# Reordering ScalarE's squares, copies and casts in the first stage of a fused recurrence and mixture-of-experts kernel

## The chip, the cores and the metric

The kernel runs on one NeuronCore of a Trainium2 chip. The metric is the device time of one execution in microseconds (us), taken as the median of several executions.

## The reference

A linear recurrence with complex decay feeds a mixture of experts that is normalised by eight rounds over rows and columns. Shapes: batch 4, 8 heads, 768 positions, head size 48; 3072 tokens of width 384, 8 experts with 1024 hidden units.

```python
scale = np.minimum(mag, 0.999) / (mag + 1e-06)      # mag = |a|
for t in range(S):
    new_re = ar * S_re - ai * S_im
    new_im = ar * S_im + ai * S_re
    S_re, S_im = (new_re + einsum('bhd,bhe->bhde', k_t, v_t), new_im)
    y[:, :, t] = einsum('bhd,bhde->bhe', q_t, S_re)
...
logits = x @ w_gate                                  # x is y with the heads side by side
P = np.exp(logits - logits.max())
for _ in range(8):
    P /= P.sum(1, keepdims=True) + 1e-09
    P /= P.sum(0, keepdims=True) + 1e-09
    P *= N / E
for e in range(E):
    out += P[:, e:e + 1] * (np.maximum(x @ w1[e], 0.0) @ w2[e])
```

## The kernel before, in words

The 3072 tokens are cut into 12 blocks of 256 (two chunks of 128 each; `SUB`, `CH`). The kernel has two stages. The first one (`phase1` and the start of `phase2a`, to about 610 us) computes the recurrence block by block and beside it the experts 0 and 1; the second (`phase2b`) the other six experts for all tokens. The change touches the first stage alone.

For each block i, `elem(i)` prepares the decay on ScalarE and VectorE: `chain` takes a *first square* (L520, with a sum), two roots and squares (L526, L527, L530) with VectorE steps between (L525 to L533), `scan` forms running products (L437 to L442, VectorE), and then a *second square* (L541), a root and its square (L545, L547), and VectorE steps (L543, L550 to L554) scale keys (kh) and queries (z). The blocks 0 to 2 do this in two halves, the others in one piece. The scaled tensors go through DMAs (L577: keys on SP, queries on GpSimd's queue) into the layouts `ks` and `qs`.

`mix(i)` is the recurrence over a block. TensorE transposes keys (ktp, L597; copied to `kts` by ScalarE, L598), multiplies them with queries (sp, L624; masked by VectorE into `sc`, L627), forms the state's increment (up, L608; copied by ScalarE as `ut`, L610; turned back as U, L617) and the output y (L641). Small ScalarE copies (rr, rn; L654 to L656) and VectorE steps (L669 to L680) carry the state on. ScalarE casts y to `xh` (L684), VectorE takes the rest `xl` (L685).

While block i goes through `mix`, the experts 0 and 1 run on block i-1, in 16 steps f of 15 matmuls: 9 into `ph` (L256), 6 into the two banks `po` (L217 to L219), which lag three steps behind. ScalarE makes `hh` from ph (L270 for blocks 0 and 1, where TensorE subtracts it again, L273, and ScalarE reads the rest, L274; for the others hh L279 and hf L280, and VectorE's hl, L281). After eight steps ScalarE copies the two banks out (`yst`, L225), and the next expert's first step may write them.

TensorE's order is written out by the program. ScalarE, VectorE, GpSimd and SP get theirs from the framework's scheduler, and the program steers it with edges that hold back an instruction without a wait on the chip: `issue_after(x)` and `add_manual_dep(b, a)` put an instruction behind x or a in the order. Each engine then works strictly in its order.

The gate stands at the end of the first stage, in `phase2a`: logits to P (L718 on GpSimd), a maximum over all (L748, mp L752), and rounds of row sums, a column sum on TensorE (cp, L784, from `spare` of L780) and rescaling (L785 to L793). Between them `more(k)` sends k steps of the last block's experts. Weights for the second stage are prepared there too (`raw` loads, GpSimd's sums L905, ScalarE's and VectorE's parts L942 and L946).

```python
more((4, 4, 2, 2)[k])
...
self.columns(self.psK.tile([128, E], F32, tag="po", name=f"cp{k}"))
```

## Time and profile before

| | |
|---|---|
| median of three executions | 1722.88 us (1721.53 to 1723.43) |
| the profiled execution | 1721.06 us |
| its span in the trace | 1719.3 us (1.76 us lie around it) |
| granted TensorE clock | 0.999 of full speed |

In the page and the views, PE is TensorE, DVE VectorE, ACT ScalarE, POOL GpSimd, SP the queue of loads. L12 is line 12 of the kernel before. In a timeline a row has the start and the length in us, the engine, the line, the operation, what it writes and reads, how many were merged (x2), and in brackets how long the engine sat idle before it and what released it. A wait that the table of waits lists is idle time of TensorE, put down to the instruction that released it. One row can hold merged neighbours, and the lengths of neighbours on one engine overlap a little, so starts say more than lengths.

### The profile page before, as it was taken

The numbers are of one execution on the slowest core, as the hardware profiler recorded it, in microseconds if no ns is written. First come the engines' busy times: TensorE is split into PE (matmuls) and PEld (weight loads), VectorE is DVE, ScalarE is ACT, GpSimd is POOL, SyncE is SP. The second block draws the span as 40 slices with busy tenths as digits, with TensorE's granted clock in tenths as the row PEclk, the third lists the DMA queues.
The fourth block names the chain that finished last, engine by engine and source line by source line (L and its number), as shares of the span: only waits on it lengthen the run. The fifth ranks groups of instructions, "written<-read, shape, count | busy, mean of one in ns | idle before, by whom it ended". The sixth has DMA issues, their size and how long they took to land.

```text
span 1719.3 us, 31262 instructions
## 1 busy us (share of the span) xinstructions
PE 1691.2 (98%) x11824; PEld 1661.2 (97%) x11824; DVE 1262.1 (73%) x2654; ACT 737.7 (43%) x1669; POOL 202.4 (12%) x383
## 2 busy tenths in 40 slices
PE   7999999999999999999999999999999999999998
PEld 5899999999999999999999999999999999999998
DVE  7898999999988787878755666656566655565654
ACT  8555555555543454645433333333433333433331
POOL 4210112111201324242200000000000000000000
PEclk9999999999999999999999999999999999999999
DMA  7434444644448877576577666558666656656560
GB/s 229 134 107 145 118 128 121 167 114 114 115 136 271 350 284 284 213 292 234 199 260 250 224 219 249 192 203 275 226 218 237 205 177 243 232 191 236 192 228 35
DMA packets 160830, 346.02 MB, mean 201 GB/s; under 512 B 15264, under 2 KB 101536, under 8 KB 160672
## 3 DMA queue, kind: packets, MB, share of 16 engines
q1 hardware_dynamic: 155264, 334.03, 56.4%
q0 software_dynamic: 4608, 9.52, 2.5%
q8 instruction: 95, 1.56, 0.4%
q14 instruction: 63, 0.52, 0.1%
q10 hardware_dynamic: 800, 0.39, 0.1%
HBM read 232.53 MB, written 98.70 MB: 193 GB/s over the span
## 4 chain that ended last, share of the span: by engine, by line
PE 67%; DVE 2%; DMA 1%; issue 0%; ACT 0%; POOL 0%; POOLq 0%; SPq 0%; DVEq 0%
PE po L1100 12%; PE po L1098 12%; PE po L1099 12%; PE X L1154 4%; PE X L1155 4%; PE X L1156 4%; PE Y L1154 3%; PE Y L1155 3%; PE Y L1156 3%; PE ph L256 1%; PE V L1154 1%; PE Z L1154 1%; PE V L1156 1%; PE V L1155 1%; PE Z L1155 1%; PE Z L1156 1%
## 5 line engine op out<-in xcount | busy, mean ns | idle before, releaser
L1100 PE MATMUL po<-wd,hl 128*128 128x384 f32 x768 | 257.0, 335 | 0.0
L1099 PE MATMUL po<-wd,hh 128*128 128x384 f32 x768 | 256.6, 334 | 0.0
L1098 PE MATMUL po<-wd,hh 128*128 128x384 f32 x768 | 256.5, 334 | 0.0
L256 PE MATMUL ph<-xh,w 128*128 128x256 f32 x1152 | 226.2, 282 | 1.3 <-ACT xh L684 1.2
L256 PEld LDWEIGHTS ph<-xh,w 128*128 128x128 f32 x1152 | 185.3, 189 | 1.8 <-ACT xh L684 1.8
L256 PE MATMUL ph<-xl,w 128*128 128x256 f32 x576 | 154.4, 282 | 0.0
L1100 PEld LDWEIGHTS po<-wd,hl 128*128 128x128 f32 x768 | 144.2, 188 | 0.8 <-DVE hl L1176 0.2
L1098 PEld LDWEIGHTS po<-wd,hh 128*128 128x128 f32 x768 | 144.2, 188 | 0.0
L1099 PEld LDWEIGHTS po<-wd,hh 128*128 128x128 f32 x768 | 144.2, 188 | 0.0
L279 ACT ACTIVATE hh<-ph 128x256 fp32r<-128x256 f32 x160 | 61.2, 383 | 187.9 <-PE ph L256 187.3
L217 PE MATMUL po<-w,hh 128*128 128x384 f32 x384 | 137.0, 357 | 1.5 <-ACT yst L225 1.5
L219 PE MATMUL po<-w,hl 128*128 128x384 f32 x384 | 129.4, 337 | 0.5 <-DVE hl L281 0.5
L218 PE MATMUL po<-w,hh 128*128 128x384 f32 x384 | 129.1, 336 | 0.0
L1099 PE MATMUL po<-wc,hh 128*128 128x384 f32 x384 | 128.3, 334 | 0.0
L1098 PE MATMUL po<-wc,hh 128*128 128x384 f32 x384 | 128.3, 334 | 0.0
L1100 PE MATMUL po<-wc,hl 128*128 128x384 f32 x384 | 128.3, 334 | 0.0
L577 POOL DMA_DIRECT2D qs<-z x144 | 75.6, 533 | 270.5 <-DVE z L554 74.0
L1175 ACT ACTIVATE hh<-X 128x384 fp32r<-128x384 f32 x64 | 31.5, 492 | 176.1 <-PE X L1156 176.1
L256 PEld LDWEIGHTS ph<-xl,w 128*128 128x128 f32 x576 | 105.7, 189 | 0.0
L1081 DVE SCALAR_TENSOR_TENSOR oa<-po,P,oa 128x384 f32<-128x384 f32 x120 | 72.9, 613 | 20.7 <-PE po L1100 20.5
L281 DVE TENSOR_TENSOR hl<-hf,hh 128x256 fp32r<-128x256 f32 x160 | 68.0, 427 | 11.0 <-ACT hf L280 9.8
L217 PEld LDWEIGHTS po<-w,hh 128*128 128x128 f32 x384 | 72.7, 189 | 2.9 <-ACT yst L225 2.0
(1832 smaller groups left out, 4381.2 us busy)
## 6 DMA issues: line engine op xcount, KB each, us to landing
wd<-wd SPq DMA_DIRECT2D x58, 768.0 KB, 5.8
wa<-wd SPq DMA_DIRECT2D x42, 768.0 KB, 4.5
wb<-wd SPq DMA_DIRECT2D x42, 768.0 KB, 5.8
wc<-wd SPq DMA_DIRECT2D x42, 768.0 KB, 4.5
xP<-xf SPq DMA_DIRECT2D x60, 384.0 KB, 4.5
raw<-in_w_dram SPq DMA_DIRECT2D x12, 1152.0 KB, 8.7
wd<-wc SPq DMA_DIRECT2D x16, 768.0 KB, 4.2
wd<-wa SPq DMA_DIRECT2D x16, 768.0 KB, 4.1
```

Source lines behind the costliest of these rows:

```text
L217: nc.tensor.matmul(po[k], hh[:, s], w2h, start=f == 0, stop=False)
L218: nc.tensor.matmul(po[k], hh[:, s], w2l, start=False, stop=False)
L219: nc.tensor.matmul(po[k], hl[:, s], w2h, start=False, stop=f == NF - 1)
L256: nc.tensor.matmul(ph, w[:, k, ct * 128:ct * 128 + 128], x[:, ct, :], start=q == 0, stop=q == len(terms) - 1)
L577: dma = eng.dma_start(dst[q:q + D - 2:NCT, :, :w], src[:, a, ct * NCH + c, :w])
L1081: V.scalar_tensor_tensor(oa[u, k], p, self.P[:, tt, e:e + 1], oa[u, k], ALU.mult, ALU.add)
L1098: nc.tensor.matmul(po[k], hh[:, s], w2[0], start=c == 1, stop=False)
L1099: nc.tensor.matmul(po[k], hh[:, s], w2[1], start=False, stop=False)
L1100: nc.tensor.matmul(po[k], hl[:, s], w2[0], start=False, stop=c == NF)
L1154: nc.tensor.matmul(ps, w[:, 0, k], x[:, 0], start=start, stop=False, skip_group_check=True)
L1155: nc.tensor.matmul(ps, w[:, 0, k], x[:, 1], start=False, stop=False, skip_group_check=True)
L1156: nc.tensor.matmul(ps, w[:, 1, k], x[:, 0], start=False, stop=True, skip_group_check=True)
```

## The change

The change adds edges for the scheduler. On ScalarE: in block 1's second part (i = 1, n = 5) hh of step 5 goes ahead of the second half of block 1's second square, and one root of block 1 behind hh of step 6; in block 2's (i = 2, n = 3 and 4) the same for steps 3 and 4 of the next expert. The two halves of block 2's first square go behind the last steps of expert 0. The first squares of the blocks 4 and 5 go behind the bank copies yst of expert 1 on the blocks 1 and 2, and their VectorE reader behind VectorE steps of the block before. The second square of block 4 goes behind the cast xh of block 3's second chunk, that of block 10 behind the copy ut of block 9's first chunk, and a root of block 11 behind a bank copy of expert 0 on block 8. In the gate three steps instead of four stand ahead of the first column sum, so that each of the first four column sums stands one step earlier on TensorE, and the memset of `pad` is issued at the end of the rounds.

```diff
@@ -222,7 +222,7 @@
                         st = self.st.tile([128, 2, C], F32R, tag="st", name=f"yst{e}_{i}_{k}").bitcast(F32)[:, 0]
                     else:
                         st = self.xp.tile([128, C], F32, tag="yst", name=f"yst{e}_{i}_{k}")
-                    nc.scalar.activation(st, po[k], AF.Copy)
+                    self.yst[e, i] = nc.scalar.activation(st, po[k], AF.Copy)
                     nc.sync.dma_start(self.ye_d[e][i * NCH + k], st)
 
         while True:
@@ -318,6 +318,7 @@
             nc.gpsimd.memset(t, 0.0)
         self.sb = sb[:, :H * D].rearrange("p (h d) -> p h d", h=H)
         self.xs, self.vt, self.kqd, self.ql, self.sqs, self.zl, self.post = {}, {}, {}, {}, {}, {}, {}
+        self.yst, self.xhc, self.utc = {}, {}, {}
         self.ev, self.dve, self.act, self.root, self.hh, self.hl, self.nthird = [], {}, {}, {}, {}, {}, 0
         ns = self.N // SUB
         self.moe, self.lg, self.mid = self.experts(), None, []
@@ -394,8 +395,12 @@
                 for _ in range(min(len(splits), (0, 1, 2, 2).count(n))):
                     splits.pop(0)()
                 if i == 1 and n == 5:
-                    for a, b in ((self.hl[0, 4], self.post[1][1]), (self.hh[0, 5], self.root[1, 0][1])):
+                    for a, b in ((self.hl[0, 4], self.hh[0, 5]), (self.hh[0, 5], self.post[1][1])):
                         tc.add_manual_dep(b.ins, a.ins.name, edge, reason="step inside the chain")
+                if i == 1 and n == 6:
+                    tc.add_manual_dep(self.root[1, 1][0].ins, self.hf.ins.name, edge, reason="step inside the chain")
+                if i == 2 and n in (3, 4):
+                    tc.add_manual_dep((self.post[2][1] if n == 3 else self.root[2, 1][0]).ins, self.hf.ins.name, edge, reason="step inside the chain")
                 if i == 1 and n == 4:
                     for ins in self.post[1]:
                         tc.add_manual_dep(ins.ins, self.hf.ins.name, edge, reason="chain behind the step")
@@ -414,6 +419,7 @@
                 pairs.append([t[k] for k in range(5) for t in (n0, n1)] + self.dve["m", NCH][:1] + n0[5:] + n1[5:])
                 a0, a1 = self.act[2, 0], self.act[2, 1]
                 pairs.append([t[k] for k in range(4) for t in (a0, a1)])
+                pairs += [[self.hh[0, 7], a0[0]], [self.hh[0, 8], a1[0]]]
                 pairs += [[a1[k], self.hh[0, n]] for k, n in ((1, 12), (2, 13), (3, 14))] + [[a1[2], self.act["kt", 1, 0][0]]]
                 for order in pairs:
                     for a, b in zip(order, order[1:]):
@@ -510,20 +516,25 @@
         base = 2 * ns + ns * NCT * NCH
         z = zt[:, :, :, :CH]
         sq, x, y0, zz = alloc("sq"), alloc("x"), alloc("y0"), alloc("zz")
-        prev = {2: (1, NCH - 1), 3: (2, NCH - 1)}.get(i)
+        prev = (i - 1, NCH - 1 if i <= NHALF else 0) if 1 < i < 6 else None
         for n in parts or [None]:
             f0, f1 = (base + i, base + NHALF + i) if n else (i, ns + i)
             sq_, x_, y_, zz_, z_ = (t if n is None else half(t, n) for t in (sq, x, y0, zz, z))
             with ExitStack() as st:
                 if prev:
                     st.enter_context(tc.issue_after(self.sqs[prev].ins))
+                if i in (4, 5):
+                    st.enter_context(tc.issue_after(self.yst[1, i - 3].ins))
                 act = self.act[i, n or 0] = [nc.scalar.activation(sq_, z_, AF.Square, accum_out=fl[:, f0:f0 + 1])]
             ops = self.dve[i, f"n{n or 0}"] = []
             with ExitStack() as st:
                 if prev:
-                    st.enter_context(tc.issue_after(self.zl[prev[0], 3 - i if i > 2 else 1].ins))
+                    st.enter_context(tc.issue_after((self.zl[prev[0], 3 - i if i > 2 else 1] if i <= NHALF else self.dve[prev][2]).ins))
                 ops.append(V.scalar_tensor_tensor(x_, sq_[:, 0], 1e-20, sq_[:, 1], ALU.max, ALU.add))
-            act.append(nc.scalar.activation(y_, x_, AF.Abs_reciprocal_sqrt))
+            with ExitStack() as st:
+                if i == ns - 1:
+                    st.enter_context(tc.issue_after(self.yst[0, i - 3].ins))
+                act.append(nc.scalar.activation(y_, x_, AF.Abs_reciprocal_sqrt))
             act.append(nc.scalar.activation(zz_, y_, AF.Square, accum_out=fl[:, f1:f1 + 1]))
             ops.append(V.tensor_tensor(x_, x_, zz_, ALU.mult))
             ops.append(V.scalar_tensor_tensor(y_, x_, -3.0, y_, ALU.add, ALU.mult))
@@ -538,7 +549,12 @@
         sq, x, g0, kh = alloc("sq"), alloc("x"), alloc("g0"), alloc("kh")
         for n in parts or [None]:
             sq_, x_, g_, z_, qk_, kh_ = (t if n is None else half(t, n) for t in (sq, x, g0, z, qk, kh))
-            act = nc.scalar.activation(sq_, z_, AF.Square)
+            with ExitStack() as st:
+                if i == 4:
+                    st.enter_context(tc.issue_after(self.xhc[i - 1, NCH - 1].ins))
+                if i == ns - 2:
+                    st.enter_context(tc.issue_after(self.utc[i - 1, 0].ins))
+                act = nc.scalar.activation(sq_, z_, AF.Square)
             self.post.setdefault(i, []).append(act)
             self.dve[i, f"x{n or 0}"] = [V.scalar_tensor_tensor(x_, sq_[:, 0], 1e-26, sq_[:, 1], ALU.max, ALU.add)]
             o = 2 * ns + i * NCT * NCH + (n or 0) * NCT
@@ -607,7 +623,7 @@
                         q = 64 * g
                         nc.tensor.matmul(up[q:q + n, j, :], vt[:, c, lo:lo + n], self.kts[:, 4 * g + j, :], start=True, stop=True, tile_position=(0, q), skip_group_check=True)
                 ut["s"] = tmp.tile([SK, 4, SK], F32, tag="tm", name=f"ut{i}_{c}", bufs=1)
-                nc.scalar.activation(ut["s"], up, AF.Copy)
+                self.utc[i, c] = nc.scalar.activation(ut["s"], up, AF.Copy)
 
             def back(i=i, c=c, ut=ut, lastc=lastc):
                 if lastc:
@@ -681,7 +697,7 @@
                 self.ist = 1 - self.ist
 
             def cast():
-                nc.scalar.activation(xh[:, :, cs], xp, AF.Copy)
+                self.xhc[i, c] = nc.scalar.activation(xh[:, :, cs], xp, AF.Copy)
                 ops.append(nc.vector.tensor_tensor(xl[:, :, cs], xp, xh[:, :, cs].bitcast(F32), ALU.subtract))
 
             if c < NCH - 1:
@@ -990,13 +1006,13 @@
         self.sums(0)
         for nm in FORMS:
             self.swap(0, nm)
-        nc.gpsimd.memset(xa.tile([128, 56], F32, name="pad"), 0.0)
+        pad = xa.tile([128, 56], F32, name="pad")
         self.sinkhorn(xa, more, True)
         for k in range(HEAD):
             self.rows()
             if k == HEAD - 1:
                 break
-            more((4, 4, 2, 2)[k])
+            more((3, 4, 2, 2)[k])
             if k == 2:
                 self.verdict()
                 more(1)
@@ -1008,6 +1024,8 @@
             if k == 0:
                 self.sums(1)
                 self.raw_w(2)
+        with tc.issue_after(self.hf.ins):
+            nc.gpsimd.memset(pad, 0.0)
         more(len(todo))
         self.moe.send((None, None, None))
```

Three places in ScalarE's order show what moves. The numbers behind names are block and chunk (xh4, y4_1, ut9_0) or expert, block and step (hh1_3_7), and the last one is the buffer's; lines of the changed kernel lie 16 further down in `chain` and `mix` behind L541 (L541 becomes L557, L684 becomes L700), L520 becomes L528.

First, ScalarE in block 1's second square, around 71 us; before:

```order
L541 ACTIVATE sq1_884<-z1_777 128x6x128
L274 ACTIVATE hl0_0_4_1023<-ph0_0_4_1012 128x256
L541 ACTIVATE sq1_884<-z1_777 128x6x128
L270 ACTIVATE hh0_0_5_1043<-ph0_0_5_1033 128x256
L545 ACTIVATE g01_886<-x1_885 128x3x128
```

and with the change:

```order
L557 ACTIVATE sq1_884<-z1_777 128x6x128
L274 ACTIVATE hl0_0_4_1023<-ph0_0_4_1012 128x256
L270 ACTIVATE hh0_0_5_1043<-ph0_0_5_1033 128x256
L557 ACTIVATE sq1_884<-z1_777 128x6x128
L561 ACTIVATE g01_886<-x1_885 128x3x128
```

hh of step 5 has moved ahead of the second half of the square.

Second, ScalarE between the last two steps of expert 1 on block 3 and the cast of block 4's second chunk, around 245 us. This place is not named in the change; before:

```order
L545 ACTIVATE g05_3576<-x5_3575 128x768
L546 ACTIVATE fl_82<-x5_3575 128x6
L520 ACTIVATE sq6_4128,fl_82<-z6_4122 128x1536
L547 ACTIVATE g05_3576<-g05_3576 128x768
L279 ACTIVATE hh1_3_7_3403<-ph1_3_7_3393 128x256
L280 ACTIVATE hf1_3_7_3405<-ph1_3_7_3393 128x256
L526 ACTIVATE y06_4130<-x6_4129 128x768
L610 ACTIVATE ut4_1_3421<-up4_1_3412 112x448
L527 ACTIVATE zz6_4131,fl_82<-y06_4130 128x768
L684 ACTIVATE xh4_3165<-y4_1_3342 128x3x128
```

and with the change:

```order
L557 ACTIVATE sq5_3574<-z5_3477 128x1536
L279 ACTIVATE hh1_3_7_3403<-ph1_3_7_3393 128x256
L280 ACTIVATE hf1_3_7_3405<-ph1_3_7_3393 128x256
L626 ACTIVATE ut4_1_3421<-up4_1_3412 112x448
L561 ACTIVATE g05_3576<-x5_3575 128x768
L562 ACTIVATE fl_82<-x5_3575 128x6
L528 ACTIVATE sq6_4128,fl_82<-z6_4122 128x1536
L563 ACTIVATE g05_3576<-g05_3576 128x768
L700 ACTIVATE xh4_3165<-y4_1_3342 128x3x128
L537 ACTIVATE y06_4130<-x6_4129 128x768
```

The second square of block 5 (sq5) stood four rows ahead of the first piece and now stands behind hh of step 6; root, square and root of the blocks 5 and 6 (g05, sq6, g05) stood ahead of hh1_3_7 and now stand between ut and xh; the root and square of block 6 (y06, zz6) now follow xh.

Third, ScalarE around the second chunk of block 9, around 455 us; before:

```order
L541 ACTIVATE sq10_6895<-z10_6798 128x1536
L610 ACTIVATE ut9_0_6509<-up9_0_6500 112x448
L684 ACTIVATE xh9_6372<-y9_0_6386 128x3x128
L545 ACTIVATE g010_6897<-x10_6896 128x768
L546 ACTIVATE fl_82<-x10_6896 128x6
L520 ACTIVATE sq11_7491,fl_82<-z11_7485 128x1536
L547 ACTIVATE g010_6897<-g010_6897 128x768
L279 ACTIVATE hh1_8_1_6555<-ph1_8_1_6545 128x256
L280 ACTIVATE hf1_8_1_6557<-ph1_8_1_6545 128x256
L598 ACTIVATE kts_211<-ktp9_1_0_6574 128x8x48
L598 ACTIVATE kts_211<-ktp9_1_1_6579 128x8x48
L654 ACTIVATE rr1_216<-qs1_196 48x8
```

and with the change:

```order
L626 ACTIVATE ut9_0_6509<-up9_0_6500 112x448
L557 ACTIVATE sq10_6895<-z10_6798 128x1536
L700 ACTIVATE xh9_6372<-y9_0_6386 128x3x128
L279 ACTIVATE hh1_8_1_6555<-ph1_8_1_6545 128x256
L280 ACTIVATE hf1_8_1_6557<-ph1_8_1_6545 128x256
L614 ACTIVATE kts_211<-ktp9_1_0_6574 128x8x48
L561 ACTIVATE g010_6897<-x10_6896 128x768
L562 ACTIVATE fl_82<-x10_6896 128x6
L528 ACTIVATE sq11_7491,fl_82<-z11_7485 128x1536
L614 ACTIVATE kts_211<-ktp9_1_1_6579 128x8x48
L670 ACTIVATE rr1_216<-qs1_196 48x8
L671 ACTIVATE rr1_216<-qs1_196 48x8
```

ut has moved ahead of block 10's second square, and g010 and block 11's first square (sq11) have moved from ahead of hh1_8_1 to a place between the two copies kts. The bank copies yst follow the rows rr and rn in both; before, the root y011 of block 11 stood between them, and now it stands behind hh and hf of the next step.

## Rows read from the trace of the kernel before

**Rows 1.** The page's part 1, busy us (share of the span) and instructions of each engine.
```profile
PE 1691.2 (98%) x11824; PEld 1661.2 (97%) x11824; DVE 1262.1 (73%) x2654; ACT 737.7 (43%) x1669; POOL 202.4 (12%) x383
```

**Rows 2.** The waits of TensorE: waited for, us in total, times, longest us.
```profile
PE mp L752 <- DVE spare L748: 1.7, 1, 1.7
PE ph L273 <- ACT hh L270: 1.6, 2, 0.9
PE po L217 <- ACT yst L225: 1.5, 2, 1.2
PE ph L256 <- ACT xh L684: 1.2, 1, 1.2
PE cp L784 <- DVE spare L780: 1.0, 2, 0.7
...
PE U L617 <- ACT ut L610: 0.6, 1, 0.6
```

**Rows 3.** Busy us (instructions) of PE, PEld, DVE, ACT, POOL, clock, DMA, 250-300 us.
```profile
250.00:300.00 50.00, 50.00 (x475) 48.59 (x474) 48.85 (x105) 26.01 (x66) 8.65 (x17) 1.00 0.48 133
```

**Rows 4.** Timeline of ScalarE from 70 us: start, length, engine, line, operation.
```profile
70.78 0.84 ACT L541 ACTIVATE sq<-z 128x768 f32<-128x768 f32 x1
71.53 0.37 ACT L270 ACTIVATE hh<-ph 128x256 fp32r<-128x256 f32 x1
```

**Rows 5.** Timeline of ScalarE around 160 and 200 us, squares and bank copies.
```profile
158.15 1.48 ACT L520 ACTIVATE sq<-z 128x1536 f32<-128x1536 f32 x1
...
199.88 1.48 ACT L520 ACTIVATE sq<-z 128x1536 f32<-128x1536 f32 x1
...
207.31 1.01 ACT L225 ACTIVATE yst<-po 128x384 f32<-128x384 f32 x2
```

**Rows 6.** Timeline of ScalarE around 245 us.
```profile
242.50 0.85 ACT L545 ACTIVATE g<-x 128x768 f32<-128x768 f32 x1 [0.56 <-DVE x L543]
...
244.82 0.83 ACT L547 ACTIVATE g<-g 128x768 f32<-128x768 f32 x1
...
248.06 0.49 ACT L684 ACTIVATE xh<-y 128x384 fp32r<-128x384 f32 x1
```

**Rows 7.** Timeline of TensorE at 249 us.
```profile
249.06 1.59 PE L256 MATMUL ph<-xh,w 128*128 128x256 f32 x12
```

**Rows 8.** Timeline of VectorE around 201 and 240 us; in brackets idle time before.
```profile
201.47 0.96 DVE L525 SCALAR_TENSOR_TENSOR x<-sq 128x768 f32<-128x768 f32 x1 [2.14 <-ACT sq L520]
...
238.60 0.34 DVE L442 TENSOR_TENSOR z<-cm_a,cm_b 128x186 f32<-128x186 f32 x1
...
243.18 1.37 DVE L627 COPY_PREDICATED sc<-spare,sp 128x512 f32<-128x512 uint8 x2
```

**Rows 9.** VectorE's groups by line, 203 to 239 us: busy, mean | idle before.
```profile
L281 DVE TENSOR_TENSOR hl<-hf,hh 128x256 fp32r<-128x256 f32 x14 | 5.8, 421 | 0.8 <-ACT hf L280 0.7
```

**Rows 10.** Timeline of ScalarE at 460 us.
```profile
459.79 0.47 ACT L225 ACTIVATE yst<-po 128x384 f32<-128x384 f32 x1
```

**Rows 11.** Timeline of TensorE from 457 us.
```profile
456.92 0.82 PE L597 MATMUL ktp<-ident,kh 128*128 128x128 f32 x6
...
460.50 0.42 PE L217 MATMUL po<-w,hh 128*128 128x384 f32 x1
```

**Rows 12.** Timeline of VectorE in the gate, 586 to 596 us.
```profile
586.07 0.17 DVE L785 TENSOR_SCALAR spare<-cp 128x8 f32<-128x8 f32 x1 [1.12 <-PE cp L784]
...
586.98 0.35 DVE L793 TENSOR_TENSOR P<-P,spare 128x192 f32<-128x192 f32 x1
...
595.92 0.62 DVE L793 TENSOR_TENSOR P<-P,spare 128x192 f32<-128x192 f32 x1
```

**Rows 13.** Line L577 (query and key transfers), issues from 298 to 301.3 us.
```profile
L577 POOL DMA_DIRECT2D qs<-z x7: 528/531/531, 298.1 to 301.2; - x7
...
DMA to landing us min/median/max: 2.7/3.3/4.2
```

**Rows 14.** Timeline of TensorE at 307 us.
```profile
306.99 0.83 PE L624 MATMUL sp<-qs,ks 112*128 112x128 f32 x6
```

## The prediction

> **What bounds the kernel now.** The page's busy times come first: TensorE (PE) works 98% of the span, VectorE (DVE) 73%, ScalarE (ACT) 43% [rows 1]. An edit of ScalarE's order can pay only where TensorE waits for something in that order, and the table of TensorE's waits, read next, says where: the lines that the change aims at (L273 for hh, L217 for yst, L256 for xh, L784 for the column sums, L617 for ut) hold 1.6, 1.5, 1.2, 1.0 and 0.6 us, 5.9 in all [rows 2]. That is all that its targets can give, 0.34% of the time. The windows show the second limit: from 250 to 300 us TensorE does not wait at all, and VectorE is busy 48.85 of 50 us [rows 3]. What is won before that must not arrive where VectorE is the late one. Last come the timelines around each wait.
>
> The profiled execution took 1721.06 us, the median of the three timed ones is 1722.88, 1.82 more. I make the sum as a difference against the profiled one and apply it to the median. Less than 0.2% (3.4 us) cannot be told from no change.
>
> **First half, up to 203 us.** *Step 5 of block 0's experts, step 3 of block 1's.* ScalarE works in order. The second half of block 1's square (L541) starts at 70.78 and hh 0.75 later [rows 4]; TensorE waits 0.9 for that hh [rows 2]. The change swaps the two: -0.75. Both halves of block 2's square run ahead of an hh in the same way; the other 0.7 of L273's 1.6 is this one. There hh moves ahead of the second half, again about 0.75 earlier, but TensorE now comes 0.75 earlier too, while the first half still starts when VectorE's scan of that block lets it go. If that scan gains nothing, 0.7 is waited again; if it gains as much, nothing is. I take the middle: -1.15 for both (ends -0.75 and -1.6).
>
> *Block 4's first square.* L520 runs for 1.48 us at 158.15 [rows 5], ahead of two bank copies yst for which TensorE then waits 1.2 [rows 2]. It goes behind them, and its reader L525 stands in VectorE's new order behind L550 to L552, so nobody misses it: -1.2 (the other end 0, if L547, still ahead of the copies, is late instead).
>
> *Block 5's first square.* The same 1.48 at 199.88 [rows 5] is ahead of the cast xh, for which TensorE waits 1.2 [rows 2]; it goes behind yst of block 2 at 207.31. The cast then comes when y is done: -1.2 (other end -0.3, if the bank copies that follow it become late). The first half gives **-3.55**.
>
> **Block 5's cast, 245 us: a wait that was not there.** The change names block 4's second square, not block 5's, but the scheduler turns the order around block 5's too (second place in the section on the change). Before, xh ended at 248.55, and TensorE wanted it at 249.06 [rows 6, 7]. In the new order L545, L520 and L547 stand ahead of xh: the pattern that cost 1.2 at 202. All hang on VectorE, whose part of block 5's scan ended with L442 at 238.94 [rows 8]. TensorE will want xh 3.55 earlier, at 245.5. If VectorE gains nothing: two ops (L669, L685) move ahead of that L442, so the scan ends at 239.9; then three state products, hl, two sc (1.37 [rows 8]) and st, 3.9 us, come before L543, which ends at 244.75; L545 to L547 is 2.32 from start to start, then 0.73 and xh's 0.49 [rows 6]: 248.3, a wait of 2.8. If VectorE gains all, sc waits for sp, L543 ends at 241.9, ut goes first, and xh ends at 246.1: a wait of 0.6. What can VectorE gain? Its idle time for hl between 203 and 239 is 0.8 us [rows 9], and of the 2.14 that it sat at 201.47 for block 5's square [rows 8] about 0.8 goes, since L550, ready when L547 is done, now comes first. So 1.6, and xh at 246.7: **+1.2**.
>
> **Blocks 10 and 11, 452 to 462 us.** ut moves ahead of block 10's square: -0.6 [rows 2]. The root L526 leaves the place between the bank copies, the first of which ran at 459.79 [rows 10]: -0.3, the rest of L217's 1.5. But L545 and L520 now stand between the two copies kts, ahead of rr and both yst. The first kts needs ktp, which TensorE starts at 456.92 [rows 11], now 0.6 earlier, and three of its six transposes: kts at about 456.85. After its 0.37, L545 and L520 with its sum read take 2.3 [rows 6]; the second kts and the three small copies rr and rn take about 1, and yst ends near 461.0. Its reader at 460.50 [rows 11] comes 0.6 earlier and waits 1.1 to 1.3. Net **+0.3** (ends -0.9 with no new wait, +1.2 if the old ones stay beside it).
>
> **The gate, 574 to 612 us.** The first four column sums stand one expert step earlier on TensorE. VectorE sat 1.12 us at L785 for the first [rows 12], so its chain starts earlier by that much or more, and the step put behind the fourth covers the wait before the fifth, 0.7 of the 1.0 [rows 2]; the wait before the fourth moves along with its chain. Against it stands GpSimd: L793 took 0.35 us with GpSimd idle and 0.62 beside its sums (L905) [rows 12], and the first round now falls nearer to the first sums. That lengthens the chain to the second product by 0.3: **-0.4** (ends -1.0; +1.2 if the sums, which wait for a load, hold the chain where it was and TensorE waits half of a step). The Trainium skill (SBUF — State Buffer, Who interferes with whom) says that a VectorE instruction with two SBUF inputs contends with a GpSimd instruction that reads SBUF; L793 agrees, and by this rule each such op of the round (the subtractions L946 and hl as well) would lengthen, the gate would give about 0, and the sum would be 0.4 higher.
>
> The GpSimd memset of the pad is written later in the program but keeps its place in the queue, ahead of the same addition, so the 1.7 before mp [rows 2] stays. The order of loads on SP shifts by a few rows; no wait in this stretch names a load, so this costs nothing, and a weight that came late would show as a new wait for a DMA.
>
> **Sum:** -3.55 + 1.2 + 0.3 - 0.4 = -2.45: 1718.6 against the profiled execution, **1720.4** against the median. This case's own range, with its ends not all on one side, is 1718.3 to 1723.3.
>
> **Rivals.** *A, the new waits don't come:* block 5's cast and the bank copies at 460 are in time. For it: VectorE is only one of two suppliers there, and its idle 2.14 could go whole. Then -3.55 - 0.9 - 0.7 = -5.15: 1717.7. Against it: both new orders are written out, and the sums are plain.
> *B, VectorE sets the pace:* at 48.85 of 50 [rows 3] it gives the first half's 3.55 back in small waits for sc, xh and hl; only -0.1 remains: 1722.8, no change.
> *C, block 6's queries come late (slower).* Block 5's first square moves from 199.88 behind the copies at 207.31, which end at 208.3 [rows 5]: 8.4 us. If VectorE cannot fill that hole and the delay rides through its queue to block 6, the transfers qs follow. Seven go out from 298.1 to 301.2 and land after 3.3, at most 4.2 [rows 13]; sp starts at 306.99 [rows 14], 2.3 us behind the typical landing. A delay of x costs x - 2.3 + 3.55 there, in place of the 1.2; with the rest, the total is x - 2.4. It decides from 2.4 us of delay, is beyond 0.2% from 5.8, and at the full 8.4 gives +6.0, 1728.9. Against it: the new order puts L550 to L554 into the hole.
> *D, the edits don't do what they say:* the orders show every named instruction moved, so it has no chance of its own.
>
> **Numbers.** Forecast 0.48, A 0.32, B 0.11, C 0.09. Faster: nearly all of A and a fifth of the forecast, 0.40. Slower: most of C and a few bad ends of the forecast, 0.09. The rest is 0.51. The range reaches to A at the bottom, 1717.2, and halfway to C at the top, 1724.6.
>
> **What would show it.** Right: L217's wait for yst near 161 and L256's for xh near 202 are gone, L273 holds about 0.5 instead of 1.6, a new wait of 1 to 2 us for xh stands near 243 and one for yst near 458, and one column sum waits instead of two. Wrong: no wait at block 5's cast (A); many small waits between 200 and 300 (B); a wait of sp for a DMA near 303 (C); a longer wait before mp.

## The result, and the profile after

The changed kernel takes 1736.82 us (median of 4 executions, 1735.8 to 1737.51) against 1722.2 (1721.32 to 1723.43) for the kernel before on the same chip: ratio 1.0084, interval 1.0072 to 1.0096. It is 14.6 us slower where 1720.4 was forecast. The profiled execution took 1737.11 us, its span is 1735.2, the granted clock 0.995.

The rows of this section are the changed kernel's where nothing else is said; the lines that were L541 to L784 stand 16 higher in it (L577 is L593, L624 is L640). Busy times, as in [rows 1]: every engine runs as many instructions as before, TensorE and GpSimd each 5 us longer.

```profile
PE 1696.3 (98%) x11824; PEld 1665.3 (96%) x11824; DVE 1263.8 (73%) x2654; ACT 737.8 (43%) x1669; POOL 207.5 (12%) x383
```

The waits of TensorE, as in [rows 2] (waited for, us in total, times, longest):

```profile
PE sp L640 <- DMA qs<-z: 9.0, 1, 9.0
PE mp L768 <- DVE spare L764: 2.4, 1, 2.4
...
PE po L217 <- ACT yst L225: 1.4, 2, 1.1
...
PE y L657 <- DVE st L696: 1.1, 2, 0.6
PE ph L256 <- ACT xh L700: 1.1, 1, 1.1
...
PE ph L273 <- ACT hh L270: 0.7, 2, 0.5
PE cp L800 <- DVE spare L796: 0.2, 1, 0.2
```

The old targets did shrink: hh 1.6 to 0.7, the column sum 1.0 to 0.2, U gone; the waits for yst near 161 and xh near 202 are gone too. In their place stand a single wait of 9.0 us for the queries of block 6, new waits for xh, st and yst, and mp is 2.4 where it was 1.7. So two of the prediction's signs of being wrong came: a wait of sp for a DMA, and a longer wait before mp. GpSimd's timeline shows what the 9.0 is made of; after:

```profile
257.83 4.48 POOL L734 TENSOR_TENSOR P<-lt_s 128x16 f32<-128x16 f32 x1 [37.12 <-ACT lt_s L733]
262.26 6.25 POOL L593 DMA_DIRECT2D qs<-z  x12
303.16 4.19 POOL L734 TENSOR_TENSOR P<-lt_s 128x16 f32<-128x16 f32 x1 [34.64 <-DVE hl L281]
307.30 6.24 POOL L593 DMA_DIRECT2D qs<-z  x12
```

and before, for the same blocks 5 and 6:

```profile
257.69 6.26 POOL L577 DMA_DIRECT2D qs<-z  x12 [35.15 <-PE lt L715]
263.96 0.45 POOL L718 TENSOR_TENSOR P<-lt_s 128x16 f32<-128x16 f32 x1
298.06 6.26 POOL L577 DMA_DIRECT2D qs<-z  x12 [33.65 <-DVE x L531]
304.33 0.56 POOL L718 TENSOR_TENSOR P<-lt_s 128x16 f32<-128x16 f32 x1
```

Two things happened. The small addition to P now stands ahead of the transfers, and there it takes over 4 us instead of about 0.5. And the queries themselves are late: the last step of block 6's z ended at 297.4 before, at 302.8 now. That step, before:

```profile
295.65 1.75 DVE L554 TENSOR_TENSOR z<-z,qk 128x1536 f32<-128x1536 f32 x1
```

and after:

```profile
301.04 1.75 DVE L570 TENSOR_TENSOR z<-z,qk 128x1536 f32<-128x1536 f32 x1
```

The first sp of block 6 needs the first six of the block's twelve qs transfers. They are issued from 307.3 instead of 298.1, and the sixth lands at 315.8 instead of 303.6. Of these 12.2 us the late z makes 5.4 and the addition 3.9. The other 2.9 lie in the sixth transfer itself, which lands 5.9 us after its issue where it took 3.0: it goes out at 309.90, right behind a load of qk that SP issues at 309.64 and that before came 4 us after it (304.83 against 300.67). That the two get in each other's way is not shown by a run of its own.

After the wait TensorE's clock is down (columns: window, its length, PE busy with the number of matmuls, clock, DMA share, GB/s):

```profile
316.00:318.00 2.00, 1.58 (x7) 0.50 0.20 39
318.00:320.00 2.00, 2.00 (x9) 0.50 0.28 60
320.00:322.00 2.00, 2.00 (x13) 0.60 1.06 304
322.00:324.00 2.00, 2.00 (x17) 1.00 0.11 29
```

From matmul to matmul against the trace before, TensorE is 1.2 us ahead at 182 us (block 3's sp), 2.7 at 229, 0.6 at 271; 9.4 behind at the first sp of block 6 and 11.9 at the second, which came 3.0 us later in the trace before; these 2.5 us are the slow clock's. It is 13.1 behind at 556, 15.9 at the second stage's first matmul (625.5 for 609.5) and 15.0 from 612 us to the last.

### The profile page after: what moved, and what is told of

Read it like the earlier page. It is cut to its first block, busy times and chain, and to the rows that moved or that the text cites. A ratio compares the mean times of both kernels' runs of the same rounds, so it can differ in the third digit from the quotient of the medians.

```text
span 1735.2 us, 31245 instructions
## 1 busy us (share of the span) xinstructions
PE 1696.3 (98%) x11824; PEld 1665.3 (96%) x11824; DVE 1263.8 (73%) x2654; ACT 737.8 (43%) x1669; POOL 207.5 (12%) x383
## 4 chain that ended last, share of the span: by engine, by line
PE 89%; DVE 6%; ACT 2%; DMA 1%; issue 1%; POOL 0%; ACTq 0%; POOLq 0%; DVEq 0%
PE po L1118 11%; PE po L1117 11%; PE po L1116 11%; PE ph L256 10%; PE X L1172 4%; PE X L1174 4%; PE X L1173 4%; PE po L217 3%; PE po L219 3%; PE po L218 3%; PE Y L1172 3%; PE Y L1174 3%; PE Y L1173 3%; PE y L657 2%; PE sp L640 2%; PE V L1172 1%
## 5 line engine op out<-in xcount | busy, mean ns | idle before, releaser
L256 PE MATMUL ph<-xh,w 128*128 128x256 f32 x1152 | 227.7, 283 | 1.2 <-ACT xh L700 1.1
L256 PEld LDWEIGHTS ph<-xh,w 128*128 128x128 f32 x1152 | 186.7, 190 | 1.8 <-ACT xh L700 1.7
L256 PE MATMUL ph<-xl,w 128*128 128x256 f32 x576 | 155.0, 283 | 0.0
L256 PEld LDWEIGHTS ph<-xl,w 128*128 128x128 f32 x576 | 106.5, 190 | 0.0
L593 POOL DMA_DIRECT2D qs<-z x144 | 75.6, 533 | 208.6 <-PE po L219 79.4
```

Source lines behind the costliest of these rows:

```text
L256: nc.tensor.matmul(ph, w[:, k, ct * 128:ct * 128 + 128], x[:, ct, :], start=q == 0, stop=q == len(terms) - 1)
L593: dma = eng.dma_start(dst[q:q + D - 2:NCT, :, :w], src[:, a, ct * NCH + c, :w])
```

## The experiments

Theory: (1) the addition, turned ahead of the queries, and (2) a later z, by the order around the moved squares, make the 9.0; mp and the clock give the rest. Rivals: block 5's moved square alone; the gate. A hold is an edge of the change that keeps an instruction behind another. Each edit starts from the changed kernel unless it says otherwise, and each version has its own line numbers; the tiles name the same steps. In a ratio the kernel before, run on the same chip, is 1.

**e1: the addition put back behind the queries.**

```diff
+            if i in (5, 6):
+                tc.add_manual_dep(self.padd[i - 1].ins, self.qd[i].ins.name, edge, reason="addition behind the queries")
```

> The changed kernel, with the two GpSimd additions (P, L734) of the blocks 4 and 5 put behind the query transfers (L593) of the blocks 5 and 6 in GpSimd's queue; the other engines keep their order. Theory (two causes: the addition, stuck for 4.2 us behind VectorE's work, stands ahead of block 6's transfers, and the queries themselves are ready 5.4 us late): the transfers start when z is ready, near 303.2 instead of 307.3, so the wait of sp falls from 9.0 to 3 to 5 us and the time from 1736.8 to 1730 to 1733. Rival (the late square alone; the addition only fills time in which the queue waits anyway): wait 9.0 and 1736.8 as they are. Rival (the addition alone): the wait goes to under 1 us, 1723 to 1725.

1728.94 us, 1.005 (1.0033 to 1.0067): half of the loss. The addition is short again, but the transfers still start 5.3 us later than before:

```profile
303.36 6.24 POOL L596 DMA_DIRECT2D qs<-z  x12 [35.23 <-DVE hl L281]
309.61 0.29 POOL L739 TENSOR_TENSOR P<-lt_s 128x16 f32<-128x16 f32 x1
```

The wait at sp is 2.8 instead of 9.0. (For this wait the tables name rn, a ScalarE copy that reads the queries, in e1, e3 and e12, and the keys in e5, e10 and e11. In all six, rn starts 0.1 us after the sixth query transfer lands, in e1 at 309.56, and sp starts 0.3 us after rn ends.)

**e2: block 5's first square left where it was; e3: e2 and e1 together.**

```diff
-                if i in (4, 5):
+                if i == 4:
...
-        prev = (i - 1, NCH - 1 if i <= NHALF else 0) if 1 < i < 6 else None
+        prev = (i - 1, NCH - 1 if i <= NHALF else 0) if 1 < i < 5 else None
```

> The changed kernel without the edges that hold block 5's first square behind yst of block 2 (block 4's stays held). Theory: block 5's chain starts some 5 us earlier, the queries of the blocks 5 and 6 are ready 3 to 5 us earlier (near 257 and 298), and since the addition still stands ahead of the transfers, the wait of sp falls to 3 to 6 us; time 1729 to 1733; the wait for xh at 202 us may come back (1.2). Rival (the addition alone): wait stays 9.0, 1736.8. Rival (the square alone): wait gone, 1722 to 1724.

> Both edits together. Theory: the wait of sp at block 6 is under 1 us, the slow clock behind it is gone with it, and the time is 1721 to 1724, about that of before. If the wait stays over 3 us, something else makes the queries late (the order around block 5's cast, which this leaves as it is).

e2: 1736.81, 1.0082 (1.0065 to 1.0099), sp wait 9.9. e3: 1729.57, 1.0044 (1.0027 to 1.0061), sp wait 3.0. Block 6's z ends at 302.7 in both, as in the changed kernel (302.8; 297.4 before). With the other holds in place, the way of that square is not what makes the queries late.

**e4: the kernel before with the gate's part alone.**

```diff
-            more((4, 4, 2, 2)[k])
+            more((3, 4, 2, 2)[k])
```

and the memset of pad written after the loop.

> The kernel before with the gate's part alone (three steps instead of four, memset of pad issued at the end). Theory: the waits for column sums fall from 1.0 to about 0.2, the wait before mp stays near 1.7 and the clock behind it stays full, so 1721.5 to 1722.5. Rival (the gate's part lengthens the wait before mp to 2.4 as in the changed kernel, and the clock falls behind it): 1723.5 to 1726.

1721.46, 0.9999 (0.9989 to 1.0008): the gate's part does nothing that can be measured. The column sums wait 0.2 as forecast, mp 1.7 as before.

**e5: e1 with the order around block 5's cast turned back by three edges.**

```diff
+            if i == 4:
+                for p, q in ((self.post[5][0], self.hh[3, 14]), (self.dve[5, "x0"][0], self.dve["m", 9][0]), (self.root[5, 0][1], self.hh[3, 15])):
+                    tc.add_manual_dep(q.ins, p.ins.name, edge, reason="block 5 as before")
```

> The kernel of e1 (P additions of blocks 4 and 5 behind the query transfers of blocks 5 and 6), and besides ScalarE's and VectorE's order around block 5's cast put back to that of before as far as edges do it: block 5's second square ahead of that stage's hh, its two-input steps ahead of the next chunk's scaling, its first root ahead of the last hh. Theory (the rest of the queries' lateness is the order around that cast, made by block 4's held second square and the held first squares together): block 6's last step ends 2 to 5 us earlier than in e1 (302.7 there), the sp wait falls from 2.8 us to under 1, the time is 1724 to 1727. Rival 1 (block 6's z is late for its own held order, not for block 5's): its step ends still after 301, sp wait over 2, the time about 1729. Rival 2 (the slow TensorE clock after other waits carries most of what is left): sp wait gone, but the time is still over 1727.

1727.99, 1.0041 (1.0027 to 1.0055): a miss. The wait for xh at 248 is gone, but one of 1.7 us for sc stands at 244.56 in its place; z of block 6 ends at 301.6 and the sp wait is 3.6. The edges put only one of the two maskings of sc (the expectation's scalings) behind block 5's step, and did not touch block 6's stage.

**e6: no holds for blocks 4 and 5 (both first squares, block 4's second square). e7: e6 with the memset of pad behind GpSimd's last addition to P. e8: the same memset in e4.**

```diff
-        prev = (i - 1, NCH - 1 if i <= NHALF else 0) if 1 < i < 6 else None
+        prev = (i - 1, NCH - 1 if i <= NHALF else 0) if 1 < i < 4 else None
...
-                if i in (4, 5):
+                if False:
...
-                if i == 4:
+                if False:
...
-        with tc.issue_after(self.hf.ins):
-            nc.gpsimd.memset(pad, 0.0)
+        ms = nc.gpsimd.memset(pad, 0.0)
+        tc.add_manual_dep(ms.ins, self.padl.ins.name, edge, reason="memset behind the addition")
```

`padl` is the last addition to P. The last three lines are e7's and e8's.

> The changed kernel without the holds of blocks 4 and 5 (their first squares, and block 4's second square); the steps of blocks 1 and 2, of blocks 10 and 11 and the gate stay. Theory: the additions stand behind the query transfers again, block 6's last step ends near 297.4 as before, no sp wait; what stays is the mp wait of 1.7 to 2.4 us and the gains of the rest, about zero: 1719.5 to 1723. Rival (blocks 1 and 2, or 10 and 11, carry part of the loss): the time is above 1724, and the positions at 85 to 135 us or at 446 to 463 us are later than before by over 1 us.

> e6 with the memset of the tile pad moved behind the last P addition on GpSimd, so that this addition, on which mp hangs, no longer waits for the memset's release. Theory: mp's wait falls below 0.7 us, and with it the stretch of slow clock behind it if there is one; 1 to 3 us less than e6: 1718 to 1721. Rival (VectorE's spare sums end late by themselves, the memset only stands beside): mp's wait stays at 1.7 to 2.4, the time is e6's.

> The kernel before with the gate's part of the change and the memset of pad behind the last P addition. Theory: mp's wait of 1.7 us in e4 falls below 0.7, the time is 1719.5 to 1721. Rival (VectorE's spare sums end late by themselves): mp's wait stays at 1.7, the time 1721.5.

e6: 1725.6, 1.002 (1.001 to 1.003), no sp wait, z at 297.6, but mp 3.1. e7: 1723.12, 1.0007 (0.9998 to 1.0017), no wait at mp. e8: 1719.8, 0.9991 (0.9981 to 1.0), no wait at mp. The holds of blocks 4 and 5 are the whole of the late queries, and the memset stands in mp's path. A part of it only moves: e7 and e8 wait 1.5 and 2.0 us for hf (L256) instead, which neither e6 nor e4 does. The traced execution of e8 took 1722.38 us, more than its median: behind those 2.0 us the clock stands at 0.65 and 0.50 from 590 to 594 us, so the gain of the median is not seen in its trace.

**e9: e7 without the holds of blocks 10 and 11.**

```diff
-                if i == ns - 1:
+                if False:
...
-                if i == ns - 2:
+                if False:
```

> e7 without the holds of block 10's second square and block 11's first root; what is left of the change is the steps of blocks 1 and 2 and the gate, with the memset moved. Theory: the 0.9 us by which e7 is behind at 537 to 556 us, and the 1.2 us of its median over before, come from blocks 10 and 11: 1719.5 to 1721.5, as e8 (1719.8), which lacks only the steps of blocks 1 and 2. Rival (the steps of blocks 1 and 2 cost it, at the start): 1722.5 to 1724, as e7.

1720.3, 0.9991 (0.9982 to 1.0001), as e8. But the 0.9 us of lag at 537 us, which the theory gave to these holds, is still there: right on the time, wrong on the place. e4, which has none of these holds, lags 1.2 there, and e8 is 0.6 ahead. VectorE's steps up to hl, for which TensorE waits at 535 us, hang on a load; the kernel before:

```profile
532.00 0.56 DVE L807 TENSOR_TENSOR xt<-xt,xt 128x384 f32<-128x384 f32 x1 [2.23 <-DMA xt<-x_d]
```

and e4:

```profile
533.17 0.56 DVE L807 TENSOR_TENSOR xt<-xt,xt 128x384 f32<-128x384 f32 x1 [1.72 <-DMA xt<-x_d]
```

In e8 the step starts at 531.42. From 500 us to there VectorE runs the same row of instructions in all three, so up to a microsecond of lag at this place is a matter of when the load lands and no sign of an edit.

**e10, e11, e12: which of the holds?** e7 with the additions behind the queries, and held: both first squares (e10), block 4's second square (e11), block 4's first square (e12). e12's lines:

```diff
-        prev = (i - 1, NCH - 1 if i <= NHALF else 0) if 1 < i < 6 else None
+        prev = (i - 1, NCH - 1 if i <= NHALF else 0) if 1 < i < 5 else None
...
-                if i in (4, 5):
+                if i == 4:
...
-                if i == 4:
+                if False:
```

> e7 with the holds of the first squares of blocks 4 and 5 back, block 4's second square free, and the P additions of blocks 4 and 5 behind the query transfers of blocks 5 and 6. Theory (each of the holds by itself makes block 6's queries late, since either puts the order around block 5's cast as the changed kernel has it): block 6's last step ends after 301 (297.6 in e6), the sp wait is over 1.5 us, the time 1724 to 1728. Rival (block 4's held second square makes it): its step ends before 299.5, no sp wait over 0.5, and the 1.2 to 2.7 us gained up to 228 us stay: 1720 to 1722.

> e7 with block 4's second square held again and the first squares of blocks 4 and 5 free, the P additions behind the query transfers. Theory (each of the holds by itself is enough): no lead up to 228 us, block 6's last step after 301, sp wait over 1.5 us, 1725 to 1729. Rival (the first squares make it): its step before 299.5, no sp wait over 0.5, the time that of e7, 1723.

> e10 with block 5's first square free too: of the holds in the first half only that of block 4's first square. Theory: the wait for yst at 161 us is gone (1.2 us ahead at 181 us), but block 6's last step is as late as in e10: sp wait over 1.5 us, 1724 to 1728. Rival (only block 5's held square makes it late): no sp wait over 0.5, 1721 to 1722.5.

e10 1727.79, 1.0034 (1.0019 to 1.0048); e11 1730.57, 1.0048 (1.0031 to 1.0064); e12 1725.04, 1.0016 (1.0007 to 1.0026). Waits at sp 3.3, 3.4, 3.0; z of block 6 ends at 302.3, 304.2, 301.2. Each of block 4's two holds is enough by itself; block 5's was not run alone. VectorE's timeline of e12 in block 6's stage shows why:

```profile
285.45 1.36 DVE L648 COPY_PREDICATED sc<-spare,sp 128x512 f32<-128x512 uint8 x2
286.69 0.54 DVE L701 TENSOR_TENSOR st<-sa,sb 112x384 f32<-112x384 f32 x1
287.15 0.95 DVE L562 SCALAR_TENSOR_TENSOR x<-sq 128x768 f32<-128x768 f32 x1
288.02 0.75 DVE L281 TENSOR_TENSOR hl<-hf,hh 128x256 fp32r<-128x256 f32 x2
290.57 0.96 DVE L536 SCALAR_TENSOR_TENSOR x<-sq 128x768 f32<-128x768 f32 x1 [1.81 <-ACT sq L531]
```

L562 is the step from the second square on which ScalarE's root hangs, and behind that root stand the next block's first square (L531) and VectorE's L536. It runs behind two maskings of sc (which the next expectations call scalings) and the state's sum st, and VectorE, full before it, then idles 1.81 us for ScalarE's square, which stood behind that root. Before, the same step stood ahead of them:

```profile
283.85 0.96 DVE L543 SCALAR_TENSOR_TENSOR x<-sq 128x768 f32<-128x768 f32 x1
...
285.06 0.74 DVE L627 COPY_PREDICATED sc<-spare,sp 128x512 f32<-128x512 uint8 x1
285.69 0.55 DVE L680 TENSOR_TENSOR st<-sa,sb 112x384 f32<-112x384 f32 x1
...
287.29 0.96 DVE L525 SCALAR_TENSOR_TENSOR x<-sq 128x768 f32<-128x768 f32 x1 [0.39 <-ACT sq L520]
```

**f1: e12 without the holds of blocks 10 and 11, and VectorE's order put right in the stages of blocks 5 and 6; f2: the same from e10.**

```diff
+            if i in (4, 5):
+                m0, m1, x = self.dve["m", 2 * i], self.dve["m", 2 * i + 1], self.dve[i + 1, "x0"][0]
+                for p, q in ((self.dve["c"][-1], m0[2]), (x, m0[-2]), (x, m1[0]), (x, m1[1])):
+                    tc.add_manual_dep(q.ins, p.ins.name, edge, reason="step ahead of the scaling")
```

> e12 (of the first half only the hold of block 4's first square; the P additions behind the transfers, the memset late) without the holds of blocks 10 and 11, and with VectorE's order put right in the stages of blocks 5 and 6: the last steps of the scan ahead of the state's products, the second square's first step ahead of both scalings and of the state's sum. Theory (that order makes block 6's queries late): block 6's last step ends before 299 (301.2 in e12), sp wait under 0.7, the 1.4 us of lead at 181 us mostly kept to the end: 1718 to 1720.5, faster than before. Rival (the held square itself): sp wait still over 2, 1722 to 1725.

> The same with both first squares held (e10 without the holds of blocks 10 and 11, and with VectorE's order put right). Theory: block 6's last step before 299.5 (302.3 in e10), sp wait under 1, the lead of 2.8 us at 228 us in part kept: 1717.5 to 1720.5. Rival (the held squares themselves): sp wait over 2, 1724 to 1727.

f1 1721.24, 0.9993 (0.9983 to 1.0002); f2 1721.76, 0.9996 (0.9987 to 1.0006). z of block 6 ends at 296.8 and 299.0, and no wait of sp for queries is left. f1:

```profile
283.27 0.96 DVE L566 SCALAR_TENSOR_TENSOR x<-sq 128x768 f32<-128x768 f32 x1
284.15 0.75 DVE L652 COPY_PREDICATED sc<-spare,sp 128x512 f32<-128x512 uint8 x1
...
286.72 0.96 DVE L540 SCALAR_TENSOR_TENSOR x<-sq 128x768 f32<-128x768 f32 x1 [0.40 <-ACT sq L535]
```

So the late queries are that order, with the squares held all the same (wholly so in f1; z in f2 is still 1.6 later than before). The edges also put the last steps of the scan ahead of the state's products; which of the two counts for more was not separated. The lead is kept only in part: f1 is 2.3 us ahead at 229, 1.3 at 310, 0.3 at 556; both times are a little over what was expected, and neither can be told from the kernel before.

**f3: the kernel before with the gate's part and the holds of blocks 10 and 11.**

```diff
+                if i == ns - 1:
+                    st.enter_context(tc.issue_after(self.yst[0, i - 3].ins))
...
+                if i == ns - 2:
+                    st.enter_context(tc.issue_after(self.utc[i - 1, 0].ins))
```

> The kernel before with the gate's part and the holds of blocks 10 and 11, nothing else. Theory (profiles): the wait for U goes (0.75), a wait for yst and others take it back, under 0.5 us at the end: ratio 0.9995 to 1.0004 against before. Rival (the medians of e7 and e9): 2 to 3 us slower than e4, ratio 1.0011 to 1.0018.

1725.57, 1.0018 (1.0009 to 1.0028): the rival. Up to 556 us its trace is no later than e4's (1.0 and 1.2 behind the kernel before, of which the load at 535 us makes 1.0 in e4 and 0.3 in f3). The difference is at mp, which waits 2.6 us against 1.7 in e4. GpSimd, e4 and then f3:

```profile
575.97 0.14 POOL L1012 MEMSET pad<- 128x56 f32 x1 [43.04 <-ACT yst L225]
576.07 0.22 POOL L718 TENSOR_TENSOR P<-lt_s 128x16 f32<-128x16 f32 x1
```

```profile
576.69 0.14 POOL L1027 MEMSET pad<- 128x56 f32 x1 [43.23 <-DMA xf<-xsv]
576.79 0.22 POOL L733 TENSOR_TENSOR P<-lt_s 128x16 f32<-128x16 f32 x1
```

The memset reuses a buffer and is let go by the landing of a store (xf<-xsv), which SP issues at 572.38 in f3, at 571.38 in e4. (e4's row names yst, but there too the memset starts with SP's transfer xP<-xf, which needs the same landing: 575.95 in e4, 576.67 in f3.) And after the longer wait the clock falls; in e4 it stays. f3, then e4:

```profile
578.00:580.00 2.00, 2.00 (x11) 0.50 1.03 407
580.00:582.00 2.00, 2.00 (x10) 0.66 1.04 414
```

```profile
578.00:580.00 2.00, 2.00 (x14) 1.00 1.02 341
580.00:582.00 2.00, 2.00 (x16) 1.00 1.01 368
```

From mp to the first column sum f3 takes 9.5 us, e4 8.0. The other versions fit: the seven with the holds of blocks 10 and 11 and the memset ahead of the addition (the changed kernel, e1, e2, e3, e5, e6, f3) wait 2.3 to 3.1 us at mp, the two without these holds (before, e4) 1.7.

## Why the prediction was wrong

By the medians the 14.6 us are taken off in steps, each against the kernel before on its own chip: e1 is 7.4 behind, e6 3.7, e7 1.2, e9 1.9 ahead. So the addition ahead of the queries costs 7.2 (with the longer landing and the clock behind it), the holds of blocks 4 and 5 another 3.7, the memset in mp's path 2.5, the holds of blocks 10 and 11 about 3. The 3.7 are net of the lead of up to 2.7 us that the same holds gave; the order on VectorE alone is seen in the traces, where at block 6's second sp e12 is 3.3 behind and f1 1.3 ahead.

*First half.* The squares were right: TensorE is 1.2 ahead at 182 us by block 4's, another 1.5 by 229 through block 5's. At blocks 1 and 2 the waits for hh fell within the stated ends, from 1.6 to 0.7, but the lead of 0.6 at 72 us is gone at block 1's sp at 86, and that of 0.6 at 120 us by 135; forecast 1.15, worth 0. What takes it back is not shown.

*Block 5's cast, +1.2.* The wait came, but larger: st 0.6 at 244.17, xh 1.1 at 248.59 and smaller ones take 2.2 of TensorE's lead between 240 and 249 us. The text let VectorE gain 1.6 us; it gained nothing, for what was L543 ended at 244.98 where the working has 244.75 for no gain:

```profile
244.03 0.95 DVE L559 SCALAR_TENSOR_TENSOR x<-sq 128x768 f32<-128x768 f32 x1
```

*Block 6's queries, put at nothing.* The same rows, with L543 behind the maskings and the sum, were read for when xh comes and not for when block 6's z comes. VectorE has no room there [rows 3]: in block 6's stage the step ran at 288.77 instead of 283.85, VectorE then idled 1.81 us for the square behind its root, and z ended 5.4 us later. That is **the first step that failed**: the sum has no term for it. It is rival C's mechanism, "the delay rides through its queue to block 6", but C was tied to the 8.4 us of block 5's square and dismissed because L550 to L554 fill that hole. e2 shows that this square's way is not needed for it; e12 and f1 show the order that makes the delay. C's own sum, x - 2.4, would have made 3.0 us of the 5.4. (Its 2.3 us of slack was counted to the seventh transfer; the first sp needs six, and the sixth had landed 3.4 us before it.)

*GpSimd's queue.* **The second step that failed**, and the dearest. The text followed the memset and the addition on GpSimd in the gate, and not the addition past the transfers, which the same change moves. Priced at its usual 0.38 us (the median of 12) it would have seemed harmless, but at 303.16 it ran beside VectorE's unbroken row of operations with two inputs and ended only behind six of them, at 307.35. The end of that row in the changed kernel:

```profile
306.25 0.56 DVE L443 TENSOR_TENSOR cm_a<-z 128x384 f32<-128x384 f32 x1
306.72 0.55 DVE L443 TENSOR_TENSOR cm_b<-z 128x384 f32<-128x384 f32 x1
307.31 0.36 DVE L447 TENSOR_TENSOR z<-cm_a,cm_b 128x192 f32<-128x192 f32 x1
```

The Trainium skill (SBUF — State Buffer, Who interferes with whom), which the prediction used for the gate, says that a VectorE instruction with two SBUF inputs contends with a GpSimd instruction that reads SBUF. The trace agrees, in that the addition took 4.19 us here; but it took only 0.45 and 0.56 beside such operations at 263.96 and 304.33 before, so the company alone does not tell the length. The trace before had one such long addition as well, 4.479 us at 211.84, with nothing urgent behind it.

*mp, "the 1.7 stays".* It became 2.4, because the store that frees the memset's buffer comes later: it is issued at 584.23 instead of 570.16, 14.1 us later, where TensorE was 13.1 behind. The text called the order of SP's loads free of cost and did not look at its stores. The clock, which no term held, then takes 2.5 us after sp and 1.6 after mp.

*Blocks 10 and 11, +0.3.* Their direct part was near: U's wait goes (0.7 us won by 460), yst's takes it back (0.8 at 463), and another 0.5 goes at 507, which the kernels without these holds do not lose. Most of their cost in f3 is at mp, 110 us later. *The gate, -0.4:* 0.0 measured, within what can be told.

What stays open: by the ratios e7 and e9 differ by 2.8 us though neither waits at mp. Their traces show 0.6 of it at 530 us (0.8 and 0.2 behind the kernel before), and their profiled spans differ by 1.0 (1721.0 and 1720.0); no row shows the rest, so mp is not the whole price of the holds of blocks 10 and 11. The lower end of the prediction's range, 1717.2, does not follow from its working either, which puts A at 1717.7; nothing hangs on it. No version here beats the kernel before by more than its measurement: e8 and e9 come nearest, at 0.9991.

## What to carry to other kernels

Where one engine has no idle time, ask of a reordering which chain of results now starts later on it, and not only whether the engine that bounds the kernel finds its next operand; the bill came 60 us downstream. Read every queue that the scheduler has turned, GpSimd's too: an addition that mostly took 0.4 us took over 4 beside a run of VectorE's two-input operations, with urgent transfers behind it. When a wait grows, add what the slow clock behind it costs: here 1.4 to 2.5 us.

## What the runs showed of the hardware

GpSimd's addition of 128x16 elements took 0.2 to 0.6 us in most places, 1.22 once each in e12 and f1, and 4.19 and 4.48 us beside VectorE's unbroken rows. There it did not end with the VectorE instruction that it met but five or six instructions later: at 303.16 in a gap of some 0.04 us between two of them, at 257.83 and 211.84 where the profile shows no gap.

The prediction had no clock in it. Waits of 1.5 to 1.8 us left the clock at 1.00 (before and e4 at mp, e7, e9 and f1 at hf). Waits of 2.0 to 3.6 were followed by 3 to 4 us at the lower of its two levels, 0.50 of full speed (among them the changed kernel and f3 at mp, e1 and e5 at sp, e8 at hf), with one exception, the 2.3 us at mp in e5. The wait of 9.0 was followed by about 6 us at 0.50 to 0.60.
